# Loading queries, keys and values of a head pair as nine flat chunks, in a fused attention and two-layer feed-forward kernel

## The chip, the cores and the metric

One core of one Trainium2 chip. The metric is the device time of one execution in microseconds; the median of several runs is given.

Names used below: PE is the matrix engine (TensorE), PEld its loading of weights, DVE the vector engine, ACT the scalar engine, POOL the GpSimd engine, SP the engine whose queue issues all transfers (DMA) of this kernel. SBUF is the on-chip memory, PSUM the accumulators that PE writes.

## The reference

Block-causal attention over 4 batches, 8 heads, 576 tokens and head size 64 (blocks of 64 tokens), then two feed-forward layers over the 2304 tokens (512 to 2048 to 512 features):

```python
scores = scale * np.matmul(q, k.transpose(0, 1, 3, 2))
scores = np.where(block_i >= block_j, scores, -1000000000.0)
attn = np.exp(scores - max); attn = attn / (sum + 1e-09)
x = (attn @ v), heads side by side                      # 2304 x 512
h = x @ w_in;  g = max(h, 0) + alpha * min(h, 0);  x = g @ w_out
h = x @ w2_in; g = h * sigmoid(1.702 * h);         out = g @ w2_out
```

q, k and v are 32-bit floats. The four weight matrices arrive as 64-bit floats.

## The kernel before, in words

**Precision.** Each 32-bit operand of a matrix product is split into a high part (`hi_part`, line 114, on ACT) and the remainder (`lo_part`, line 117, on DVE or POOL). A layer product is then three products: high x high, low x high, high x low. Weights are narrowed from 64 to 32 bits by one ACT and three DVE instructions (`narrow`, line 137) and then split.

**Attention.** Work goes by `passes` (line 307): a pass is a pair of heads of one batch. Batch 0 is taken in eight passes: first the query group 0 (rows 0 to 319) of its four pairs, then group 1 (rows 320 to 575), so that the first token block of the layers comes early. The twelve pairs of batches 1 to 3 are one pass each, with both groups. Per pass:

- `load` (line 328) fetches rows of q, k and v through `load_rows` (line 319) into the tiles `nat`, where one partition row holds 64 values of the first head and 64 of the second. A full pair takes, for each of q, k and v, one transfer per head (128 KB, line 324) and one for the last 64 rows of both heads (line 326).
- `prep_t` (line 338) transposes 128 rows of both heads at once on PE, into `tp` in PSUM. The first head comes out on partitions 0 to 63, the second on 64 to 127.
- `prep_out` (line 347) splits that: high parts on ACT, low parts on DVE, one instruction per head. For keys, the low part goes to the other half of the partitions. For queries, both parts stay on the head's own half, and once all query parts of the pass are there, two transfers within SBUF (line 383) copy each head's half to the other half, since a score product needs the same query part against the high half and the low half of the keys.
- `prep_v` (line 385) splits v into three 16-bit parts on ACT and POOL.
- `score` (line 426) makes the products `sc`; `soft` (438) the minimum (DVE) and the exponential (ACT); `norm`, `high` (471, POOL) and `rest` (483, DVE) the normalised probabilities as two 16-bit parts `hl`. Line 493 transposes those by a DMA transpose into `pt`, one per pass, group and head: 64 in all.
- `pv` (line 496) multiplies with v by the list `PV` (line 28), one list per group; `pv_out` (518) adds the halves into `x` and stores it.

**Layers.** The first half of layer 1 (8 of 16 feature tiles) runs beside the attention, by token blocks: two of 320 and 256 tokens for batch 0, then six of 288 (`blocks`, line 595). `gemm1` (line 194) and `g2_half` (232) are its products. The rest of layer 1, and layer 2, follow when the attention's buffers have been given up, by blocks of 384 tokens (`gemm1` and `g2`, line 632). Products of `gemm1` and `g2_half` take their PSUM banks in turn from a pool of two, `ps_m`. `warm` (line 575) issues matmuls without a result on one of these two banks, in groups at steps -5 to 27 of the plan, each group ordered behind the PE instruction ahead of it in the plan.

**The order of the work.** Each piece of work is noted with `at(kind, n, fn)` (line 110): a step `n`, and a place, `n + 0.1 * ORDER[kind] + SHIFT[kind]` (line 111). After the program has been built in the order of the steps, `arrange` (line 778) simulates it with a cost per instruction: on each engine the ready instruction with the smallest place goes next. The order found is then fixed for every engine, SP's queue included. `cost` (754) prices compute instructions, lines 817 to 823 price transfers, lines 889 to 895 say how SP and the transfers follow each other. Each engine carries out its order strictly. `SHIFT` (line 44) holds one number per kind of work.

Of the kernel before, what the change touches and what calls it, by code (L numbers as in the profile page):

```python
# [27 lines left out]
PV = [  # L28
# [3 lines left out]
]  # L32
# [23 lines left out]
def kernel(  # L56
# [27 lines left out]
    NG = 6  # L84
    TB = 384
# [101 lines left out]
    gs_ = blk.tile([128, 2 * NA * GRP[0][2]], F32R, name="gs")  # L187
# [29 lines left out]
    def gate_split(key, f, lo):  # L217
        g, n = pend.pop((key, f))

        w, z = (GRP[0][2], f % NA) if key[0] == 0 else (TB, f % NG)  # L220
# [40 lines left out]
    def plan_x(i, n_split):  # L261
        def f(c):
            if c == 0:
                t0, n = blocks[i]
                xl = blk.tile([128, KD, GRP[0][2]], F32R, tag="xlb", name="xlb")[:, :, 0:n]
                xb[0, i] = (st["x", t0 // S][:, :, t0 % S:t0 % S + n], None, xl, n)
            split_x((0, i), blk, 0, pool, slice(c, c + 1))
# [12 lines left out]
    nat = {n: one.tile([128, 5, 2, D], F32, name=f"nat_{n}") for n in "qkv"}  # L280
    vp = [one.tile([128, 5, 7, D], BF16, name=f"vp{i}") for i in range(2)]
# [3 lines left out]
    def hl_part(j, x, m, n, h):  # L285
        o = 128 * (QT[j][4] + x * QT[j][3])
        z = hl[0 if j < 3 else 1]
        return z[h % len(z)][0:m, o:o + n]


    def setup():
# [4 lines left out]
        for t in nat.values():  # L296
            pool.memset(t[64:128, 4], 0.0)
        for t in vp:
            pool.memset(t[:, :, 3, :], 0.0)
# [10 lines left out]

    PART0 = ((0, 320, ((0, 128), (1, 128), (4, 64))), (320, 256, ((2, 128), (3, 128))))
    PART = ((0, 384, ((0, 128), (1, 128), (2, 128))), (384, 192, ((3, 128), (4, 64))))

    def part_of(i, part):
        return (PART0 if i < N0 else PART)[part]

    def load_rows(nm, i, t0, n, c0, tail):
        b, p, _ = passes[i]  # L320
        src = {"q": q, "k": k, "v": v}[nm][b, 2 * p:2 * p + 2]
        c = n // 128
        for h in range(2):
            sp.dma_start(out=nat[nm][:, c0:c0 + c, h], in_=src[h, t0:t0 + 128 * c, :].rearrange("(c p) d -> p c d", p=128))
        if n % 128:
            sp.dma_start(out=nat[nm][0:64, tail], in_=src[:, t0 + 128 * c:t0 + n, :].rearrange("h p d -> p h d"))

    def load(i, nm):
        gs = passes[i][2]
        if len(gs) == 2 or nm == "v" and gs[0] == 1:  # L330
            load_rows(nm, i, 0, S, 0, 4)
        elif nm == "v":
            load_rows(nm, i, 0, 384, 0, 4)
        else:
            t0, n, chunks = PART0[gs[0]]
            load_rows(nm, i, t0, n, chunks[0][0], 4)

    def prep_t(i, nm, part):
        ps = ps_a.tile([128, 512], F32, tag="tv", bufs=2, name="tp")
        st["tp", i, nm, part] = ps  # L340
        o = 0
        for c, m in part_of(i, part)[2]:

            pe.transpose(ps[:, o:o + 128], nat[nm][:, c].rearrange("p h d -> p (h d)"), ident)
            o += m

    def prep_out(i, nm, part):


        t0, n, _ = part_of(i, part)  # L350
        ps = st.pop(("tp", i, nm, part))[:, 0:n]
        if nm == "q":
            if (i, nm) not in st:
                st[i, nm] = two.tile([128, 2, 2, S], F32R, tag="q", name="qs")
            z = st[i, nm]
        elif i < N0:

            p = passes[i][1]
            if part == 0 and p == 0:
                st["k0"] = blk.tile([128, KD, S], F32R, tag="xl0", name="k0")  # L360
            if part == 0:
                st["k0", p] = st["k0"][:, 2 * p:2 * p + 2] if p < KD // 2 else two.tile([128, 2, S], F32R, tag="k", name="k0")
            z = st["k0", p]
        else:
            if (i, nm) not in st:
                st[i, nm] = two.tile([128, 2, S], F32R, tag="k", name="ks")
            z = st[i, nm]
        half = [slice(0, 64), slice(64, 128)]
        t = slice(t0, t0 + n)
        for h in range(2):  # L370
            hi = z[half[h], h, 0, t] if nm == "q" else z[half[h], h, t]
            hi_part(hi, ps[half[h]], -scale if nm == "q" else 1.0)
        for h in range(2):
            if nm == "q":
                dve.scalar_tensor_tensor(out=z[half[h], h, 1, t], in0=ps[half[h]], scalar=-scale,
                                         in1=z[half[h], h, 0, t].bitcast(F32), op0=ALU.mult, op1=ALU.subtract)
            else:
                lo_part(dve, z[half[1 - h], h, t], ps[half[h]], z[half[h], h, t])
        if nm == "q" and part == passes[i][2][-1]:
            z = z.bitcast(F32)  # L380
            t = slice(0, S) if i >= N0 else t
            for h in range(2):
                sp.dma_start(out=z[half[1 - h], h, :, t], in_=z[half[h], h, :, t])

    def prep_v(i, piece):
        n = 5 if passes[i][2][-1] == 1 else 3
        t, src = vp[i % 2], nat["v"]

        part = t[:, 0:n, piece:7 - piece:6 - 2 * piece, :]
        act.activation(out=part, in_=src[:, 0:n], func=ACTF.Copy)  # L390
        pool.tensor_tensor(out=src[:, 0:n] if piece == 0 else t[:, 0:n, 2:5:2, :], in0=src[:, 0:n], in1=part, op=ALU.subtract)
# [34 lines left out]
    def score(n):  # L426
# [4 lines left out]
        for j, off, heads, parts, _ in st[n, "sc"]:  # L431
            q0, m, nk, ch, c0 = QT[j]
            for part in parts:
                for h, (o, k0, n_) in zip(heads, part):
                    for x in range(2):
                        pe.matmul(o, qs[:, h, x, q0:q0 + m], ks[:, h, k0:k0 + n_], start=x == 0, stop=x == 1)
# [46 lines left out]
    def rest(n, h):  # L483
# [9 lines left out]
        sp.dma_start_transpose(out=pt, in_=hl[g][h % len(hl[g])])  # L493
        st[i, g, h] = pt

    def pv(i, g, h):
# [4 lines left out]
        for o, n, c, skip, tiles in PV[g]:  # L501
            first = [QT[j][4] for j in tiles]
            for a, x in (((0, 0), (0, 1), (2, 0)), ((5, 0), (5, 1), (3, 0)))[h]:
# [5 lines left out]
                ops.append((ps[:, o:o + n], t[:, c, a:a + 2].rearrange("p a d -> p (a d)"), mv))  # L509
# [34 lines left out]

    for i in range(len(passes)):
        full = passes[i][2][-1] == 1
# [7 lines left out]
        todo = [(nm, g) for g in passes[i][2] for nm in "kq"]  # L554
        for z, (nm, part) in enumerate(todo):
# [393 lines left out]
```

## Time and profile before

| what | value |
|---|---|
| median of 3 runs | 1120.61 us (1120.26 to 1124.37) |
| the profiled execution, its own time | 1119.54 us |
| its span in the profile | 1117.7 us |
| packets moved by transfers | 238,919, of which 191,984 under 512 bytes |
| bytes moved | 123.59 MB |

How to read the lines of the profile: the page gives busy time per engine, with the share of the span and the number of instructions behind an x. In groups of instructions, a line names the source line, the engine, the operation, output <- input, shapes and a count; then busy time and mean duration in ns; then the idle time just before them and what ended it. In the view of one tile, a line gives the shortest, median and longest duration in ns and the first and last start. In the view in order of time, a line starts with the start and the duration in us. A wait reads "who <- whom: us in total, times, longest us". SPq is SP's queue: the time in which it issues a transfer, which is not the transfer's own time. Tiles: `nat_q`, `nat_k`, `nat_v` are the loaded rows, `tp` the transposes, `qs` and `ks` (or `k`) the split queries and keys, `sc` the scores, `hl` and `pt` the probabilities before and after the transpose, `pv` their product with v, `h` and `x` the layer products.

The profile's strip of 40 equal slices shows the stages (28 us a slice; digits are tenths):

```profile
PE   6556888868989989899999999999999999999998
DVE  6889877768688887678987125851111111111110
PEclk7888989978999999999999999999999999999999
DMA  7878778797878776544555214511001010000000
```

The attention fills the first 16 slices. There PE, DVE and the transfers are all at 5 to 9 tenths, and the clock granted to PE is below full in the first eight. After that PE is at 9 tenths throughout, DVE falls off, and the transfers stop mattering.

### The profile page before, as it was taken

To read this page: it belongs to the slowest core of one execution; us is meant where nothing else is said; L and a number is where in the kernel's file an instruction comes from. 1 tells how busy PE (TensorE), PEld (TensorE's weight loads), DVE (VectorE), ACT (ScalarE), POOL (GpSimd) and SP (SyncE) were. 2 spreads that over 40 slices of the span, in tenths; PEclk is the share of its full clock that TensorE was granted. 3 is DMA by queue.
4 is the path that set the end of the run, shared out by engine and by line. 5 is a ranking of instruction groups with operands and counts; after the bars stand their busy time and mean duration, and the time that the engine had idled before them with its cause. 6 is when DMAs were issued, how large, how long until landed. Compare 5 with 4: busy or idle time off the path is not lost. (4 is left out here: it accounts for less than half of the span.)

```text
span 1117.7 us, 17627 instructions
## 1 busy us (share of the span) xinstructions
PE 1020.0 (91%) x6478; PEld 926.6 (83%) x6478; DVE 608.1 (54%) x1057; ACT 508.3 (45%) x1192; POOL 463.1 (41%) x496
## 2 busy tenths in 40 slices
PE   6556888868989989899999999999999999999998
PEld 3445777757878879799999999999999999999997
DVE  6889877768688887678987125851111111111110
ACT  5555655546565765555554225533223232232222
POOL 3467654635564745553443224442222222222221
PEclk7888989978999999999999999999999999999999
DMA  7878778797878776544555214511001010000000
GB/s 187 179 177 192 172 159 172 150 171 149 162 145 175 146 159 138 139 145 153 188 180 170 85 57 142 184 57 33 25 1 57 1 57 1 29 29 1 29 1 29
DMA packets 238919, 123.59 MB, mean 111 GB/s; under 512 B 191984, under 2 KB 230896, under 8 KB 238832
## 3 DMA queue, kind: packets, MB, share of 16 engines
q1 hardware_dynamic: 238832, 122.46, 45.3%
q8 instruction: 51, 0.84, 0.3%
q14 instruction: 36, 0.29, 0.1%
HBM read 62.66 MB, written 18.87 MB: 73 GB/s over the span
## 5 line engine op out<-in xcount | busy, mean ns | idle before, releaser
L118 POOL TENSOR_TENSOR gs<-g,gs 128x384 fp32r<-128x384 f32 (+3 forms) x208 | 216.6, 1044 | 456.3 <-ACT gs L115 444.8
L202 PE MATMUL h<-xh,wh 128*128 128x384 f32 (+3 forms) x832 | 272.1, 327 | 9.8 <-DVE g L211 6.8
L202 PE MATMUL h<-xh,wl 128*128 128x384 f32 (+3 forms) x832 | 270.8, 325 | 0.0
L214 DVE TENSOR_TENSOR g<-g,h 128x384 f32<-128x384 f32 x96 | 53.2, 554 | 294.8 <-ACT g L213 294.8
L649 PE MATMUL acc<-wh,gs 128*128 128x512 f32 x576 | 194.9, 392 | 0.6 <-DVE o L659 0.6
L202 PE MATMUL h<-xl,wh 128*128 128x384 f32 x576 | 193.1, 335 | 0.0
L202 PEld LDWEIGHTS h<-xh,wh 128*128 128x128 f32 x832 | 156.6, 188 | 17.8 <-DVE g L211 9.4
L202 PEld LDWEIGHTS h<-xh,wl 128*128 128x128 f32 x832 | 157.0, 189 | 0.1
L115 ACT ACTIVATE gs<-g 128x384 fp32r<-128x384 f32 (+3 forms) x208 | 103.4, 498 | 105.5 <-DVE g L214 60.1
L213 ACT ACTIVATE g<-h 128x384 f32<-128x384 f32 x96 | 47.1, 491 | 195.4 <-PE h L202 195.1
L515 PE MATMUL pv<-pt,vp 128*128 128x256 f16 (+2 forms) x1056 | 92.8, 238 | 45.1 <-DMA pt<-hl 43.5
L481 POOL TENSOR_SCALAR hl<-e,stat 64x64 f16<-64x64 f32 (+4 forms) x160 | 106.3, 681 | 63.0 <-DVE stat L469 45.3
L489 DVE SCALAR_TENSOR_TENSOR hl<-e,stat,hl 64x64 f16<-64x64 f32 (+4 forms) x160 | 120.9, 782 | 11.5 <-POOL hl L481 9.9
L649 PEld LDWEIGHTS acc<-wh,gs 128*128 128x128 f32 x576 | 108.1, 188 | 21.1 <-DVE o L659 1.0
L515 PEld LDWEIGHTS <-vp 128*128 128x128 bf16 x1056 | 65.8, 103 | 64.3 <-DMA pt<-hl 36.1
L649 PE MATMUL acc<-wl,gs 128*128 128x512 f32 x288 | 113.7, 395 | 0.0
L202 PEld LDWEIGHTS h<-xl,wh 128*128 128x128 f32 x576 | 108.1, 188 | 4.1
L649 PE MATMUL acc<-gs,wh 128*128 128x384 f32 x384 | 97.5, 334 | 2.0 <-DVE o L659 2.0
L459 ACT ACTIVATE e<-sc,stat 64x64 f32<-64x64 f32 (+4 forms) x160 | 82.7, 519 | 20.7 <-DVE stat L451 15.2
L211 DVE SCALAR_TENSOR_TENSOR g<-g,nalph,h 128x288 f32<-128x288 f32 (+3 forms) x112 | 61.4, 551 | 49.8 <-ACT g L210 48.8
L118 POOL TENSOR_TENSOR wl<-sq,wh 128x512 fp32r<-128x512 f32 x40 | 56.6, 1416 | 68.4 <-ACT wh L115 58.7
L240 PE MATMUL x<-gs,wh 128*128 128x288 f32 (+2 forms) x256 | 76.4, 302 | 4.8 <-DVE g L211 4.7
(67 smaller groups left out, 1694.8 us busy)
## 6 DMA issues: line engine op xcount, KB each, us to landing
rw<-in_moe_w_in_dram SPq DMA_DIRECT2D x32, 512.0 KB, 4.0
rw<-in_moe_w_out_dram SPq DMA_DIRECT2D x32, 512.0 KB, 3.6
qs<-qs SPq DMA_DIRECT2D x24, 288.0 KB, 4.2
o<-xa SPq DMA_DIRECT2D x24, 192.0 KB, 2.9
xl<-xs SPq DMA_DIRECT2D x6, 768.0 KB, 4.7
x2s<-o SPq DMA_DIRECT2D x24, 192.0 KB, 1.9
xl<-x2s SPq DMA_DIRECT2D x6, 768.0 KB, 4.4
out_dram<-o SPq DMA_DIRECT2D x18, 256.0 KB, 2.0
```

The costliest lines, as they stand in the source:

```text
L115: act.activation(out=dst, in_=src, func=ACTF.Copy, scale=scale_)
L118: eng.tensor_tensor(out=dst, in0=src, in1=hi.bitcast(F32), op=ALU.subtract)
L202: pe.matmul(ps, st_[:, sl], mv[:, c], start=z == 0, stop=z == 3 * KD - 1)
L211: dve.scalar_tensor_tensor(out=g, in0=g, scalar=nalph[:, f:f + 1], in1=ps, op0=ALU.mult, op1=ALU.add)
L213: act.activation(out=g, in_=ps, func=ACTF.Sigmoid, scale=1.702)
L214: dve.tensor_tensor(out=g, in0=g, in1=ps, op=ALU.mult)
L240: pe.matmul(ps, oh[:, sl], gh, start=f == 0, stop=False)
L459: act.activation(out=eo, in_=v[:, h] if len(heads) > 1 else v, func=ACTF.Exp, scale=-1.0, bias=stat[0:m, 0, a:a + 1], accum_out=stat[0:m, ...
L481: pool.tensor_scalar(out=o, in0=e, scalar1=r, scalar2=1.0, op0=ALU.mult, op1=ALU.mult)
L489: dve.scalar_tensor_tensor(out=hl_part(j, 1, m, nk, h), in0=es[h][0:m, off:off + nk], scalar=stat[0:m, 2, 2 * a + h:2 * a + h + 1], in1=hl ...
L515: pe.matmul(o, l, r, start=z == 0, stop=z == len(ops) - 1)
L649: pe.matmul(ps, a, b_, start=f == f0 and z == 0, stop=f == NF - 1 and z == 2)
```

## The change

The two heads of a pair lie one behind the other in memory, so their 2 x 576 rows are nine chunks of 128 rows, and the fifth chunk holds the end of the first head and the start of the second.

1. Loads. q, k and v are loaded as such chunks: k and v once, q twice, into the two halves of each partition row of `nat_q`. A transpose of a chunk of q then gives the same 128 queries on partitions 0 to 63 and on 64 to 127. Keys are transposed two chunks at a time. In batch 0 the passes of group 0 load and prepare all keys, and seven of nine chunks of q and v; the passes of group 1 load seven chunks of q and all of v, and no keys.
2. `prep_out`. Queries are split with all 128 partitions in one instruction per part. The two transfers of line 383 are gone. Keys are still split by halves, a half now being the even or the odd chunks.
3. The second head's rows start 64 rows into the fifth chunk. Its probabilities are therefore written 64 columns further on in `hl`, and `PV` has a second list for it.
4. Token blocks are 288 tokens throughout (`TA`); the buffer `gs` is smaller.
5. `arrange` prices transfers anew: time on SP, time of the packets and a landing time, by run length and by kind, with a DMA transpose holding SP for a time that grows with its size.
6. `SHIFT` has new numbers for every kind of work, and the steps of the loads follow the transposes that free their tiles.

```diff
-PV = [
+PV = [[
     [(0, 64, 0, 0, (0,)), (64, 256, 0, 0, (1, 2)), (128, 64, 1, 64, (1,)), (192, 128, 1, 0, (2,)), (256, 64, 2, 64, (2,))],
     [(0, 256, 0, 0, (3, 4)), (0, 256, 1, 0, (3, 4)), (0, 256, 2, 0, (3, 4)), (64, 64, 3, 64, (3,)), (128, 128, 3, 0, (4,)),
      (192, 64, 4, 64, (4,))],
-]
+], [
+    [(0, 64, 0, 0, (0,)), (64, 256, 0, 0, (1, 2)), (64, 256, 1, 0, (1, 2)), (192, 128, 2, 0, (2,))],
+    [(0, 256, 0, 0, (3, 4)), (0, 256, 1, 0, (3, 4)), (0, 256, 2, 0, (3, 4)), (0, 256, 3, 0, (3, 4)), (128, 128, 4, 0, (4,))],
+]]
...
 SHIFT = {
-    "gate": -13.8, "gate 2": 48.4, "gemm1": 60, "gemm1 2": 60, "gemm2": 60, "half": 60, "half out": -58.4,
-    "high": -53.6, "load alpha": 58.5, "load k": 20.6, "load q": 56.4, "load v": 60, "load w": -11,
-    "load w 2": -60, "load x": 46.3, "narrow": 54.9, "narrow 2": 7.4, "norm": -50, "out": -20.2,
-    "prep out": 24.8, "prep t": -17.9, "prep v": 17.6, "pv": -8.2, "pv out": 35.6, "rest": 50.5, "score": -46.6,
-    "setup": 28.7, "soft": -24.9, "split g": 20.9, "split g 2": 3.7, "split w": -48.5, "split w 2": 60,
-    "split x": 29.2, "split x 2": -44.7, "warm": 9.6,
+    "gate": -44.2, "gate 2": -23, "gemm1": 56.7, "gemm1 2": 12.5, "gemm2": 12.8, "half": 58.9, "half out": -42,
+    "high": -6.3, "load alpha": 27.7, "load k": 56.1, "load q": -37.1, "load v": -27.1, "load w": -32.6,
+    "load w 2": -53.5, "load x": -33, "narrow": 56.5, "narrow 2": -25.1, "norm": -46.2, "out": -53.7,
+    "prep out": 42.4, "prep t": 41.2, "prep v": 41.6, "pv": -10, "pv out": -41.9, "rest": 40.6, "score": 51.7,
+    "setup": -24.2, "soft": 19, "split g": -43.8, "split g 2": 4.8, "split w": 7.8, "split w 2": -28.1,
+    "split x": 26.4, "split x 2": 57.1, "warm": 56.9,
 }
...
     def load(i, nm):
+        b, p, gs = passes[i]
+        src = {"q": q, "k": k, "v": v}[nm][b, 2 * p:2 * p + 2].rearrange("h t d -> (h t) d").rearrange("(c p) d -> p c d", p=128)
+        if nm == "q":
+            c = slice(0, 9) if len(gs) == 2 else (slice(0, 7), slice(2, 9))[gs[0]]
+            for y in range(2):
+                sp.dma_start(out=nat["q"][:, c, y], in_=src[:, c])
+        elif nm == "v" or gs[0] == 0:
+            c = slice(0, 9 if nm == "k" or gs[-1] == 1 else 7)
+            sp.dma_start(out=nat[nm][:, c], in_=src[:, c])
...
+    CH = ((0, 1, 2, 3), (4, 5, 6, 7)), ((0, 1, 2), (4, 5, 6)), ((2, 3, 4), (7, 8))
...
+        if what == "k":
+
+            ts = [nat["k"][:, c:c + 2] for c in range(0, 8, 2)]
+        elif what == "tail":
+            ts = [nat["k"][:, 8:10]] + [nat["q"][:, 8]] * (len(passes[i][2]) == 2)
         else:
...
+            ts = [nat["q"][:, c] for c in chunks(i, what)]
+        for z, t in enumerate(ts):
+            pe.transpose(ps[:, 128 * z:128 * z + 128], t.rearrange("p c d -> p (c d)"), ident)
...
-        if nm == "q" and part == passes[i][2][-1]:
-            z = z.bitcast(F32)
-            t = slice(0, S) if i >= N0 else t
-            for h in range(2):
-                sp.dma_start(out=z[half[1 - h], h, :, t], in_=z[half[h], h, :, t])
...
+        hi_part(z[:, 0, t], y, -scale)
+        dve.scalar_tensor_tensor(out=z[:, 1, t], in0=y, scalar=-scale, in1=z[:, 0, t].bitcast(F32), op0=ALU.mult, op1=ALU.subtract)
...
-        todo = [(nm, g) for g in passes[i][2] for nm in "kq"]
+        todo = ["k", "q0", "q1", "tail"] if passes[i][2][0] == 0 else ["q0", "q1"]
...
-    blocks = [(0, 320), (320, 256)] + [(288 * i, 288) for i in range(2, 2 * B)]
+    blocks = [(TA * i, TA) for i in range(2 * B)]
...
-                c = (450 if list(a.ap)[0][1] > 64 else 625, size / 360 * (1 if min(dma_run(z) for z in ins + outs) >= 512 else 2))
+                run = min(dma_run(z) for z in ins + outs)
+                t = size / run * (8.3 + 0.0368 * run) / 16
+                inside = all(z.tensor.space != DRAM and not z.tensor.name.startswith("in_") for z in ins + outs)
+                c = (580 if inside else 400 if run > 512 else 500, 2 * t if inside else t, 1000 if outs[0].tensor.space == DRAM or inside else 1600)
             else:
-                c = (625, size / 32768 * 112)
+                c = (0.0046 * size - 100, size / 32768 * 130, 2400 - 0.0046 * size)
...
                 if e == "SP":
-                    t = max(now, dge)
-                    dge = t + c[0] + 60
-                    free[e] = max(now + 50, t)
-                    end = ring_end = max(t + c[0] + 650, ring_end) + c[1]
-                    if kind == "InstDmaTransposeAnt":
-                        dge = end - 877
+                    t = now
+                    free[e] = t + c[0] + 70
+                    end = ring_end = max(t + c[0] + c[2], ring_end) + c[1]
```

More of the change, by code (lines that the diff above doesn't have):

```diff
@@ L279 @@
     mk_l = one.tile([128, 128], BF16, name="mk_l")
-    nat = {n: one.tile([128, 5, 2, D], F32, name=f"nat_{n}") for n in "qkv"}
-    vp = [one.tile([128, 5, 7, D], BF16, name=f"vp{i}") for i in range(2)]
+    nat = {"q": one.tile([128, 9, 2, D], F32, name="nat_q"), "k": one.tile([128, 10, D], F32, name="nat_k"),
+           "v": one.tile([128, 9, D], F32, name="nat_v")}
+    vp = [one.tile([128, 9, 4, D], BF16, name=f"vp{i}") for i in range(2)]
     hl = [[one.tile([128, 128 * g[3]], F16, name=f"hl{j}{x}") for x in range(NHL[j])] for j, g in enumerate(GRP)]
@@ L295, in setup @@
         pool.memset(mk_l, 0.0)
-        for t in nat.values():
-            pool.memset(t[64:128, 4], 0.0)
+        pool.memset(nat["k"][:, 9], 0.0)
         for t in vp:
-            pool.memset(t[:, :, 3, :], 0.0)
+            pool.memset(t[:, :, 3], 0.0)
         for t in hl[0] + hl[1]:
@@ L328, in load @@
-    def load(i, nm):
-        gs = passes[i][2]
[L330 to L333, printed above, removed]
-        else:
[L335 to L345, printed above, removed]
@@ new lines, in prep_out @@
+    def prep_out(i, what):
+        ps = st.pop(("tp", i, what))
+        gs = passes[i][2]
+        if what in ("k", "tail"):
+            if i < N0:
+                p = passes[i][1]
+                if what == "k" and p == 0:
+                    st["k0"] = blk.tile([128, KD, S], F32R, tag="xl0", name="k0")
+                if what == "k":
+                    st["k0", p] = st["k0"][:, 2 * p:2 * p + 2] if p < KD // 2 else two.tile([128, 2, S], F32R, tag="k", name="k0")
+                z = st["k0", p]
+            else:
+                if what == "k":
+                    st[i, "k"] = two.tile([128, 2, S], F32R, tag="k", name="ks")
+                z = st[i, "k"]
+            z = z.rearrange("p h t -> p (h t)").rearrange("p (c t) -> p c t", t=128)
+            half = [slice(0, 64), slice(64, 128)]
+            y = ps.rearrange("p (c t) -> p c t", t=128)
+            if what == "k":
+                kinds = [(x, y[half[x]], slice(x, 8, 2)) for x in range(2)]
+            else:
+                kinds = [(0, y[half[0], 0:1], slice(8, 9))]
+            for x, s_, c in kinds:
+                hi_part(z[half[x], c], s_)
+            for x, s_, c in kinds:
+                lo_part(dve, z[half[1 - x], c], s_, z[half[x], c])
+        if what == "k" or what == "tail" and len(gs) == 1:
+            return
+        if (i, "q") not in st:
+            st[i, "q"] = two.tile([128, 2, 2 * S], F32R, tag="q", name="qs")
+        if what == "tail":
+            c0, y = 8, ps[:, 128:256]
+        else:
+            cs = chunks(i, what)
+            c0, y = cs[0], ps[:, 0:128 * len(cs)]
+        t = slice(128 * c0, 128 * c0 + y.shape[-1])
+        z = st[i, "q"]
+        hi_part(z[:, 0, t], y, -scale)
+        dve.scalar_tensor_tensor(out=z[:, 1, t], in0=y, scalar=-scale, in1=z[:, 0, t].bitcast(F32), op0=ALU.mult, op1=ALU.subtract)
@@ L543 @@
                 at("pv out", n + lag + 1 + h, lambda i=i, g=g, h=h: pv_out(i, g, h))
+    used = {}
     for i in range(len(passes)):
-        full = passes[i][2][-1] == 1
         f0 = first[i]
```

92 lines of the change are left out of this document (28 added, 64 removed).

## The prediction

> **What bounds the kernel now.** I read the page first, then a table by stage, then who waits for whom, then the queues.
>
> ```profile
> PE 1020.0 (91%) x6478; PEld 926.6 (83%) x6478; DVE 608.1 (54%) x1057; ACT 508.3 (45%) x1192; POOL 463.1 (41%) x496
> ```
>
> PE is the busiest engine by far, but 91% is an average. The table by stage, with cuts that I chose where the work changes (its columns after the time are PE, PEld, DVE, ACT and POOL busy us, granted TensorE clock, DMA share, GB/s), says where the missing 97.7 us lie:
>
> ```profile
> 0.00:118.00 118.00, 78.19 (x507) 53.39 (x508) 96.15 (x178) 66.72 (x168) 63.50 (x81) 0.83 0.79 181
> 118.00:288.00 170.00, 137.99 (x1103) 122.25 (x1101) 130.85 (x263) 98.42 (x281) 96.94 (x115) 0.92 0.79 160
> 288.00:458.00 170.00, 154.55 (x1353) 141.28 (x1354) 130.68 (x259) 101.60 (x289) 91.84 (x115) 1.00 0.77 155
> 458.00:508.00 50.00, 47.22 (x353) 46.30 (x351) 36.49 (x51) 30.06 (x65) 28.42 (x25) 1.00 0.48 149
> 508.00:1118.00 610.00, 602.07 (x3168) 563.40 (x3167) 213.95 (x308) 211.54 (x392) 182.39 (x162) 1.00 0.21 67
> ```
>
> From 458 us on (the attention is over) PE is busy 649.3 of 660 us, and 508 to 1118 is matrix products alone. The first of those stretches, 50 us, is the two blocks of the last batch, which cannot start before its attention ends. So the time is the end of the attention plus a fixed 660 us, and a microsecond saved or lost before 458 counts in full. Before 458, PE idles 39.8 us in the first stretch, 32.0 in the second and 15.4 in the third.
>
> In the first stretch it is worse than that, since half of the busy time is warm-up:
>
> ```profile
> L580 PE MATMUL warm<-mk_l 128*128 128x384 bf16 x174 | 39.5, 379 | 1.1 <-POOL mk_l L295 1.1
> ```
>
> and in order of time (start us, us):
>
> ```profile
> 116.86 0.98 PE L580 MATMUL warm<-mk_l 128*128 128x384 bf16 x5
> 119.01 0.31 PE L202 MATMUL h<-xh,wh 128*128 128x320 f32 x1
> ...
> 120.77 0.31 PE L202 MATMUL h<-xh,wh 128*128 128x320 f32 x1
> ```
>
> The steady first-layer products begin right behind the last warm-up matmul. The code says why: warm-up holds one of the two banks of `ps_m` until its last group, and that group is ordered behind the products of the sixth pass's probabilities. 118 us is therefore the time of six passes of attention with nothing beside them, 19.7 us each.
>
> What PE waits for (us in total, times, longest us), first before 118 us:
>
> ```profile
> PE pv L515 <- DMA pt<-hl: 20.7, 9, 6.5
> PE sc L436 <- ACT e L459: 4.8, 2, 3.8
> PE tp L344 <- DMA nat_k<-in_k_dram: 4.0, 1, 4.0
> PE sc L436 <- DMA qs<-qs: 3.6, 5, 1.3
> ```
>
> and from 118 to 458 us:
>
> ```profile
> PE pv L515 <- DMA pt<-hl: 22.8, 23, 2.8
> PE sc L436 <- DMA qs<-qs: 7.6, 18, 1.1
> ```
>
> Transfers inside the core (the DMA transposes of the probabilities, and the swaps of the query halves) end most waits. All of them go out through SP's one queue, whose issues last (min, median, max ns):
>
> ```profile
> L383 SPq DMA_DIRECT2D qs<-qs x40: 510/597/1642, 14.5 to 423.7; - x40
> L324 SPq DMA_DIRECT2D nat_q<-in_q_dram x40: 367/472/1325, 3.2 to 398.2; - x40
> L326 SPq DMA_DIRECT2D nat_q<-in_q_dram x16: 607/625/1372, 3.7 to 394.0; - x16
> L324 SPq DMA_DIRECT2D nat_k<-in_k_dram x40: 367/436/908, 1.3 to 392.4; - x40
> L326 SPq DMA_DIRECT2D nat_k<-in_k_dram x16: 607/684/1799, 1.8 to 389.2; - x16
> L324 SPq DMA_DIRECT2D nat_v<-in_v_dram x40: 381/538/1841, 4.4 to 406.1; - x40
> ...
> L326 SPq DMA_DIRECT2D nat_v<-in_v_dram x16: 595/675/1413, 10.6 to 401.2; - x16
> L493 SPq DMA_TRANSPOSE pt<-hl x64: 1282/2630/4094, 34.5 to 452.2; - x64
> ```
>
> Counts by medians: 40 swaps and 168 loads take 23.9 + 18.9 + 10.0 + 17.4 + 10.9 + 21.5 + 10.8 = 113 us of SP, the 64 transposes 168 us: 281 of 458 us before weights and stores. No engine is full (DVE 96.15 of 118 and 77% after, PE 81% and 91%, DMA 0.79), but all are high and every queue is in order.
>
> **The change part by part.**
>
> *Fewer transfers on SP.* A full pair now has 9 loads and 2 swaps, afterwards q twice, k once, v once. In the code that is 12 x 11 + 4 x 10 + 4 x 9 = 208 before and 12 x 4 + 4 x 4 + 4 x 3 = 76 after. At about 0.5 us (between the 0.436 and 0.538 of the three large kinds) 76 cost 38 us, so 75 us leave SP. If an issue grows with its packets (a 288 KB load has 2.25 times those of a 128 KB one), 1.1 us each makes 84, and 30 us leave. I take the first, since 128 KB pieces are issued faster than the 32 KB ones of L326. In the first six passes it is 58 issues against 22, some 20 us less in 118.
>
> *The swap's latency.* One pass of the first stretch:
>
> ```profile
> 49.29 0.53 PE L344 MATMUL tp<-ident,nat_q 128*128 128x128 f32 x3
> ...
> 51.84 1.33 SPq L383 DMA_DIRECT2D qs<-qs  x2
> 51.89 0.49 DVE L375 SCALAR_TENSOR_TENSOR qs<-tp,qs 64x320 fp32r<-64x320 f32 x1
> ...
> 55.78 0.28 PE L436 MATMUL sc<-k,qs 128*64 128x64 f32 x2 [0.75 <-DMA qs<-qs]
> ```
>
> The second low part ends at 52.4, the scores start at 55.8. Without the swap they can follow the low part: up to 3.4 us per pass, 20 us for six. It is not all gain: DVE is busy 96.15 us of the 118, so 100 us is about the floor of this stretch, and the keys of the second group are now prepared in the first four passes, ahead of the warm-up's end. At the start the new shifts put both loads of q, that of v and two of weights ahead of the first keys, for which PE waits 4.0 us now; one weight load and parts of k and q stood there before, so some two issues more, 1 us, against the first swap saved. I take 118 to 106, **-12 us**; bounds 0 (DVE sets the pace) and -18.
>
> *118 to 458 us.* The waits for swaps (7.6) go; what is late next is DVE's low part, which wrote the swap's source anyway, so nothing is left of them. Of the 22.8 us for the transposes I take about half, 12: SP is freer by roughly a quarter and the plan now prices an issue that blocks SP, but the transpose's own landing remains. Bounds 0 and 22.8. The clock of 0.92 inflates 138 us of PE work by 11; with denser PE work I take 4, bounds 0 and 11.
>
> *More PE work.* Transposes go from 160 to 12 x 14 + 4 x 11 + 4 x 5 = 232, and each second head's product list trades two 64-column products for one of 256 columns, three times per group. In 288 to 458 us:
>
> ```profile
> L515 PE MATMUL pv<-pt,vp 128*128 128x256 f16 x176 | 29.5, 274 | 5.8 <-DMA pt<-hl 5.7
> ...
> L515 PE MATMUL pv<-pt,vp 128*128 128x64 f16 x216 | 15.8, 193 | 0.0
> ...
> L344 PE MATMUL tp<-ident,nat_k 128*128 128x128 f32 x27 | 4.9, 280 | 0.0
> L344 PE MATMUL tp<-ident,nat_q 128*128 128x128 f32 x27 | 4.9, 273 | 0.0
> ```
>
> A transpose takes 9.8 / 54 = 0.181 us of PE. 24 of the 72 added ones lie in batch 0, under the dead time of the first stretch; the other 48 cost **+8.7**. A wide product takes 0.168 and a narrow one 0.073: 16 pairs x 2 x 3 x 0.022 = **+2.1**.
>
> *What costs nothing.* DVE and ACT treat the same columns of q and k per full pair, 128 rows deep and in three instructions rather than four; V is 576 columns rather than 640, which shortens POOL's and ACT's work, neither of which is full. Blocks of 320 + 256 become 288 + 288: the same columns. The new shifts reorder the late stage too; its PE idles 8 of 610 us, so there is nothing to gain there; DVE at 214 of 610 covers it, and if the new order breaks that cover I allow the same 8 us again as a loss, in the range only.
>
> Sum: -12 - 7.6 - 12 - 4 + 8.7 + 2.1 = -24.8, a span of 1092.9. The profiled execution took 1119.54 beside its span of 1117.7 (1.8 around it), 1.1 under the median of 1120.61. So 1092.9 + 2.9 = about **1095 us**.
>
> *The packets.* Per pair a swap moves runs of up to 4.6 KB, while a row of q is 256 bytes. By the code, loads grow from 58,368 such rows to 82,432, and 9,216 KB of swaps go.
>
> ```profile
> q1 hardware_dynamic: 238832, 122.46, 45.3%
> ```
>
> and, for the landing of a DMA transpose (median us from issue),
>
> ```profile
> pt<-hl SPq DMA_TRANSPOSE x64, 4.6
> ```
>
> The first row gives 16 x 1117.7 x 0.453 = 8101 us of single engines: 33.9 ns per packet, 67.7 ns per KB. The added 24,064 packets are at most 51 us over 16 engines, the swaps 39 us by bytes, or nearly nothing if long runs are cheap. The DMA share before 458 us moves from 0.78 to between 0.81 and 0.89. The sum above has 0 for it, since no transfer engine is full at either.
> The Trainium skill speaks against this part ("DMA: Bandwidth & Descriptors", "Why small descriptors are slow (HBM only)"): small pieces pay a fixed overhead when they come from HBM, and transfers within SBUF do not. By that rule the worse end, 0.89, holds; no row of this trace separates the two kinds.
>
> **The rivals.**
> - *Slower: the attention loses its head start on PE.* In the plan before, a score stands 46.6 steps early and a first-layer product 60 late; afterwards they are at 51.7 and 56.7, and the transposes move from -17.9 to 41.2. If one group of 12 products (119.01 to 120.77 is 1.76 us at 320 columns, so 1.58 at 288) stands ahead of the transposes and of the scores of each pair and the chain has no slack, 12 x 2 x 1.58 = 38 us return: 1133. It decides once the chain of a pair, about 28 us in 340 / 12, has less than 3 us of slack. For it: 458 is followed by a fixed 660. Against: PE at 81% and 91% waits for the chain's transfers now, not the chain for PE.
> - *No change: DVE keeps the pace*, or the large issues are slow: the first stretch gives 4, the transposes' waits stay, swaps' waits and added PE work remain: -4 - 7.6 + 10.8 = -0.8, so 1120. For it: DVE at 81% of the first stretch.
> - *Transfers become the limit:* at a share of 0.89 each of the 48 transposes of the full pairs lands later by (0.89 - 0.78) / 0.78 of the 2.0 us between the end of its issue and its landing (4.6 - 2.63), or 0.28 us: 13 us, so 1108. For it: the share is 0.77 to 0.79 in all three stretches. Against: bytes fall on balance, by 9.2 MB of swaps against 6.2 MB of rows.
> - *All of it:* -18 - 7.6 - 22.8 - 11 + 10.8 = -48.6, so 1072.
>
> **How the numbers follow.** Forecast 0.46, on its own 1080 (the waits for `pt` all gone, -11, and more of the clock, -4) to 1108 (half the first stretch's gain and half of the 12 us, +12); all of it 0.18; transfers 0.08; no change 0.12; slower 0.16. A difference under 0.5% (5.6 us) can't be told from none here. The first three lie under 1115: faster 0.72, same 0.12, slower 0.16. The range leaves out the slower case and a little below 1072: 1066 to 1127.
>
> **What would show it.** Right: steady first-layer products start near 106 us; no wait for `qs`; `nat` issues near 0.5 us; waits for `pt` from 118 to the attention's end about 11 us; the attention ends near 433 and 660 us follow; `tp` 15 us more of PE. Wrong: first-layer products still at 118 with DVE full; waits of DVE and ACT for `tp` and `sc` that grow; PE gaps in the late stage; or a DMA share near 0.9 with landings of `pt` well over 4.6 us.

## The result and the profile after

| | before | after |
|---|---|---|
| median | 1121.69 us (4 runs, 1120.26 to 1124.37) | 1086.31 us (4 runs, 1084.72 to 1087.43) |
| profiled execution, its span | 1119.54, 1117.7 | 1087.33, 1085.5 |

The ratio is 0.968, with a 95% interval of 0.9655 to 0.9706: 35 us faster. The forecast was 1095, with a range of 1066 to 1127. Of the variants below, `e_swaps_late` has a time but no usable profile: the one execution that was profiled took 2011 us, the nine others 1118 to 1123.

The table by stage for the changed kernel, cut where the last warm-up group starts and where the last product with v starts (same columns as in the prediction):

```profile
0.00:112.60 112.60, 81.49 (x519) 56.38 (x520) 92.29 (x172) 62.52 (x160) 63.54 (x81) 0.86 0.85 190
112.60:421.50 308.90, 285.13 (x2397) 264.55 (x2395) 256.87 (x500) 191.40 (x549) 189.22 (x226) 0.99 0.84 163
421.50:1086.00 664.50, 654.79 (x3543) 613.32 (x3540) 255.09 (x358) 240.75 (x457) 209.68 (x188) 1.00 0.23 73
```

and the kernel before, with the same two cuts:

```profile
0.00:117.50 117.50, 77.69 (x504) 52.92 (x505) 95.65 (x178) 66.25 (x167) 63.00 (x81) 0.83 0.79 182
117.50:458.10 340.60, 293.14 (x2459) 264.09 (x2457) 262.02 (x522) 200.50 (x570) 189.28 (x229) 0.96 0.78 158
458.10:1118.00 659.90, 649.18 (x3519) 609.61 (x3516) 250.44 (x358) 241.60 (x456) 210.81 (x187) 1.00 0.23 74
```

The first stretch is 4.9 us shorter, the second 31.7. The rest runs to the span's end: 1117.7 - 458.1 = 659.6 before and 1085.5 - 421.5 = 664.0 after, 4.4 longer. That makes up the 32.2 us between the two spans. Nearly all of the gain is in the second stretch: there PE's idle time fell from 47.5 to 23.8 us and its busy time from 293.1 to 285.1, while the granted clock rose from 0.96 to 0.99. The busy time did not vanish: it rose by 3.8 us in the first stretch and by 5.6 in the last, where 24 more of PE's instructions now stand, so over the whole kernel it is 1.4 us longer.

What PE waits for in the changed kernel, in the second stretch:

```profile
PE pv L519 <- DMA pt<-hl: 6.4, 7, 2.2
PE sc L441 <- ACT e L464: 5.2, 9, 1.3
PE h L207 <- ACT xo L251: 3.2, 4, 1.1
PE x L245 <- ACT wh L120: 2.4, 1, 2.4
```

The wait for swaps is gone, and the wait for transposed probabilities (`pt`) went from 22.8 to 6.4 us. These are 7.6 + 16.4 = 24.0 us of waits, and PE's idle time in this stretch fell by 23.7. What is late next is small and spread over several engines. In the first 112 us it is the loads, DVE and small things:

```profile
PE tp L345 <- DMA nat_k<-in_k_dram: 5.1, 3, 2.6
PE pv L519 <- DMA pt<-hl: 4.2, 2, 4.0
PE tp L345 <- DVE stat L473: 3.7, 1, 3.7
PE tp L345 <- DMA nat_q<-in_q_dram: 3.5, 2, 2.5
```

The wait for `pt` fell here as well, from 20.7 to 4.2 us, and the swaps' 3.6 us are gone, yet the stretch is only 4.9 us shorter. Other waits took their place, those for DVE above all: all of them together went from 0.6 to 9.8 us. The waits for `nat_k` and `nat_q` were there before (4.0 us, and the line below) and grew only from 6.7 to 8.6.

```profile
PE tp L344 <- DMA nat_q<-in_q_dram: 2.7, 1, 2.7
```

SP's issues in the changed kernel (min, median, max ns):

```profile
L322 SPq DMA_DIRECT2D nat_q<-in_q_dram x40: 368/454/3537, 0.7 to 365.1; - x40
...
L325 SPq DMA_DIRECT2D nat_k<-in_k_dram x16: 367/399/713, 2.4 to 359.3; - x16
...
L325 SPq DMA_DIRECT2D nat_v<-in_v_dram x20: 367/493/1712, 1.2 to 363.8; - x20
...
L498 SPq DMA_TRANSPOSE pt<-hl x64: 1274/2670/4946, 28.3 to 413.9; - x64
DMA to landing us min/median/max: 3.6/4.6/8.3
```

There are 76 loads with medians of 0.40 to 0.49 us (45.2 us in all). By the medians, a load of 288 KB takes SP no longer than one of 128 KB did, as assumed. A transpose still lands after 4.6 us, although the share of the transfer engines in the second stretch rose from 0.78 to 0.84.

PE's own work, the three groups that the change touches, before and after:

```profile
L515 PE MATMUL pv<-pt,vp 128*128 128x256 f16 (+2 forms) x1056 | 92.8, 238 | 45.1 <-DMA pt<-hl 43.5 <-DVE g L211 0.7 <-DVE x L528 0.6
...
L344 PE MATMUL tp<-ident,nat_q 128*128 128x128 f32 x80 | 17.0, 315 | 2.1 <-DVE ks L118 1.9 <-PE sc L436 0.2
L344 PE MATMUL tp<-ident,nat_k 128*128 128x128 f32 x80 | 16.1, 303 | 7.4 <-DMA nat_k<-in_k_dram 4.0 <-DMA nat_q<-in_q_dram 2.7 <-PE sc L436 0.5
```

```profile
L519 PE MATMUL pv<-pt,vp 128*128 128x256 f16 (+2 forms) x960 | 88.1, 248 | 14.6 <-DMA pt<-hl 10.5 <-DVE x L532 1.6 <-DVE k L123 0.8
...
L345 PE MATMUL tp<-ident,nat_q 128*128 128x128 f32 x152 | 27.6, 290 | 12.8 <-DVE stat L473 3.7 <-DMA nat_q<-in_q_dram 3.5 <-issue 2.5
...
L345 PE MATMUL tp<-ident,nat_k 128*128 128x128 f32 x80 | 15.3, 292 | 6.3 <-DMA nat_k<-in_k_dram 5.1 <-DVE x L532 0.8 <-DVE qs L388 0.2
```

The 72 more transposes cost 42.9 - 33.1 = 9.8 us, and the products with v, 96 fewer and wider, take 4.7 us less rather than more. Both sums hold a share of the higher granted clock.

### The profile page after: what moved, and what is told of

Same layout as the page of the kernel before. It is cut to its first block, busy times and chain, and to the rows that moved or that the text cites. A ratio compares the mean times of both kernels' runs of the same rounds, so it can differ in the third digit from the quotient of the medians.

```text
span 1085.5 us, 17180 instructions
## 1 busy us (share of the span) xinstructions
PE 1021.4 (94%) x6454; PEld 934.3 (86%) x6454; DVE 604.3 (56%) x1029; ACT 494.7 (46%) x1164; POOL 462.4 (43%) x494
## 5 line engine op out<-in xcount | busy, mean ns | idle before, releaser
L123 POOL TENSOR_TENSOR gs<-g,gs 128x384 fp32r<-128x384 f32 (+1 forms) x208 | 212.8, 1024 | 452.4 <-ACT gs L120 431.8
L207 PE MATMUL h<-xh,wh 128*128 128x384 f32 (+1 forms) x832 | 272.2, 327 | 6.8 <-ACT xo L251 3.7
L207 PE MATMUL h<-xh,wl 128*128 128x384 f32 (+1 forms) x832 | 270.2, 325 | 0.0
L120 ACT ACTIVATE gs<-g 128x384 fp32r<-128x384 f32 (+1 forms) x208 | 103.3, 498 | 106.7 <-DVE g L219 60.9
L519 PE MATMUL pv<-pt,vp 128*128 128x256 f16 (+2 forms) x960 | 88.1, 248 | 14.6 <-DMA pt<-hl 10.5
L464 ACT ACTIVATE e<-sc,stat 64x64 f32<-64x64 f32 (+4 forms) x160 | 82.8, 520 | 34.0 <-DVE hl L494 19.2
L216 DVE SCALAR_TENSOR_TENSOR g<-g,nalph,h 128x288 f32<-128x288 f32 (+1 forms) x112 | 61.6, 551 | 58.4 <-ACT g L215 57.4
L123 POOL TENSOR_TENSOR wl<-sq,wh 128x512 fp32r<-128x512 f32 x40 | 59.5, 1488 | 61.7 <-ACT wh L120 61.6
L245 PE MATMUL x<-gs,wh 128*128 128x288 f32 x256 | 75.7, 302 | 2.9 <-ACT wh L120 2.4
```

The source lines that it names most:

```text
L120: act.activation(out=dst, in_=src, func=ACTF.Copy, scale=scale_)
L123: eng.tensor_tensor(out=dst, in0=src, in1=hi.bitcast(F32), op=ALU.subtract)
L207: pe.matmul(ps, st_[:, sl], mv[:, c], start=z == 0, stop=z == 3 * KD - 1)
L216: dve.scalar_tensor_tensor(out=g, in0=g, scalar=nalph[:, f:f + 1], in1=ps, op0=ALU.mult, op1=ALU.add)
L245: pe.matmul(ps, oh[:, sl], gh, start=f == 0, stop=False)
L464: act.activation(out=eo, in_=v[:, h] if len(heads) > 1 else v, func=ACTF.Exp, scale=-1.0, bias=stat[0:m, 0, a:a + 1], accum_out=stat[0:m, ...
```

## The experiments

Two theories at the start. **D**, the data path: the gain comes from what is no longer done (swaps in front of the scores, small transfers on SP). **P**, the plan: it comes from the new shifts and transfer prices, which place each instruction where its transfer has landed. A third question was what sets the length of the first stretch. "Old" and "new plan" below mean shifts and prices together. Each ratio is to the kernel before on the same chip at the same time, where it took 1121.7 to 1123.7 us.

| kernel | median us | ratio (95%) | last warm-up starts | last product with v starts |
|---|---|---|---|---|
| before | 1121.7 | 1 | 117.5 | 458.1 |
| after | 1086.3 | 0.968 (0.9655 to 0.9706) | 112.6 | 421.5 |
| e_old_plan | 1098.4 | 0.979 (0.9756 to 0.9819) | 115.7 | 424.4 |
| e_before_new_plan | 1158.7 | 1.033 (1.0289 to 1.0360) | 140.0 | 492.2 |
| e_swaps | 1166.8 | 1.040 (1.0369 to 1.0437) | 145.0 | 498.5 |
| e_swaps_old_plan | 1169.3 | 1.041 (1.0380 to 1.0440) | 140.8 | 509.3 |
| e_swap_by_part | 1162.8 | 1.036 (1.0334 to 1.0385) | 131.5 | 494.6 |
| e_swap_by_part_old_plan | 1141.6 | 1.018 (1.0155 to 1.0196) | 137.5 | 477.6 |
| e_swaps_late | 1120.6 | 0.997 (0.9960 to 0.9987) | no profile | no profile |
| e_split_loads | 1098.9 | 0.979 (0.9765 to 0.9823) | 115.5 | 430.2 |
| e_head_start | 1102.1 | 0.981 (0.9786 to 0.9833) | 117.9 | 428.6 |
| e_jitter | 1107.2 | 0.987 (0.9850 to 0.9888) | 128.3 | 443.0 |
| e_short_warm | 1093.6 | 0.975 (0.9731 to 0.9768) | 68.2 | 421.3 |
| e_no_narrow | 1081.8 | 0.964 (0.9621 to 0.9657) | 116.0 | 412.4 |

### Plan and data path exchanged

`e_old_plan` is the changed kernel with the `SHIFT` table and the transfer prices of the kernel before; `e_before_new_plan` is the kernel before with those of the changed kernel. Core of the first edit:

```diff
-                c = (580 if inside else 400 if run > 512 else 500, 2 * t if inside else t, 1000 if outs[0].tensor.space == DRAM or inside else 1600)
+                c = (450 if list(a.ap)[0][1] > 64 else 625, size / 360 * (1 if min(dma_run(z) for z in ins + outs) >= 512 else 2))
...
-    "gate": -44.2, "gate 2": -23, "gemm1": 56.7,
+    "gate": -13.8, "gate 2": 48.4, "gemm1": 60,
```

> The changed kernel's data path (nine-chunk loads, queries twice, no swaps, blocks of 288) with the shifts and the transfer prices of the kernel before; nothing of the computation differs. Theory D (the data path gives the gain: swaps and 132 transfers gone from SP): most of the 35 us stays, 1086 to 1100. Theory P (the plan gives it: new shifts and prices put each instruction where its transfer has landed): the gain is lost, 1115 to 1135, with waits for pt back near 20 us after the first stretch.

> The kernel before (swaps, nine loads per pair, blocks of 320 and 256) with the shifts and the transfer prices of the changed kernel. Theory D: it stays within 10 us of 1121, since swaps and small loads are still there. Theory P: it comes down to 1090 to 1105, with the waits for pt falling as they did in the changed kernel (27 to 10 us less).

Measured: 1098.4 and 1158.7. The data path under the old plan keeps 24 of the 35 us; the new plan alone, on the old data path, loses 36. Theory P falls as the main cause: its plan is worse than the old one for a kernel that swaps. That it does something for the new data path (12 us) is measured against the control below.

### The swaps put back

In the changed kernel both halves of the partitions hold the same queries, so a swap can be put back that writes what is there already. In `e_swaps` it stands in `prep_out`, behind the last query part and ahead of the scores:

```diff
+        if what == ("tail" if len(gs) == 2 else "q1"):
+            swap(i)
...
+    def swap(i):
+        z = st[i, "q"].bitcast(F32)
+        gs = passes[i][2]
+        t0, n = (0, S) if len(gs) == 2 else GRP[gs[0]][1:3]
+        for h in range(2):
+            c = slice(S * h + t0, S * h + t0 + n)
+            sp.dma_start(out=z[64 - 64 * h:128 - 64 * h, :, c], in_=z[64 * h:64 * h + 64, :, c])
```

> The changed kernel with the two swap transfers of each pass put back ahead of the scores (they write the values that are there already, so the output is the same), planned with the new prices. Theory D: 40 more issues (24 us of SP), 9.4 MB more and the swap's landing in front of every score cost 15 to 25 us: 1100 to 1112. Theory P: the plan works around them, 1086 to 1093.

`e_swaps_old_plan` is the same under the old plan:

> The changed data path with the swaps put back ahead of the scores, and the shifts and prices of the kernel before (it differs from the run with the old plan by the swaps alone; they write values that are there already). If the swap is dear by itself (its issue, its bytes and its landing in front of the scores), it costs 15 to 25 us here too: 1113 to 1123. If it was dear only because the new plan gives the scores no head start, it costs under 8 us here: below 1106.

Measured: 1166.8 and 1169.3, that is 80 and 71 us over the kernels without swaps, far more than either theory expected. Part of it may be this edit: cut by head, in a tile that has the head inside the part, the second transfer overlaps the first in the planner's rectangles, and under the old plan the order of SP's queue showed 5.7 us between the two issues of the first pass (at 15.61 and 21.29 us). So the swap was cut by part instead, both transfers from the lower to the upper half, with the same bytes and the same number of issues:

```diff
+        for x in range(2):
+            w = z[:, x].rearrange("p (h t) -> p h t", t=S)[:, :, t0:t0 + n]
+            sp.dma_start(out=w[64:128], in_=w[0:64])
```

> As the run with the swaps put back, with the new plan, but the two transfers of a pass are cut by part (high, low) rather than by head: both copy partitions 0 to 63 to 64 to 127, so that neither has rows in common with the other, which the earlier cut had and which put the second swap behind the first in the plan. The same bytes and the same number of issues; the output is unchanged. If the 80 us were mostly the swaps' own cost: still over 1140. If half of it or more was the two swaps one after the other: 1100 to 1130.

> The same swaps by part, with the shifts and prices of the kernel before; to be set against 1098 without swaps. Theory D (swap issue, bytes and landing in front of the scores are the main cost of the kernel before): 1113 to 1128, close to the 1122 of the kernel before. If the small loads are what costs: below 1108. If the earlier cut was no matter: 1160 or more.

Measured: 1162.8 and 1141.6, so 76 us over the changed kernel and 43 over `e_old_plan`. The earlier cut cost 28 us under the old plan, but only 4 under the new one, so it was the cause of little there. The expected 15 to 30 us were too few, and the new plan suffers more from a swap than the old. The kernel so made is not the kernel before, though: under the old plan it is 20 us slower than that one, which swaps too. So the 43 us are what a swap costs in this data path; they are not the swaps' share of the 35 us gained. The waits of PE in `e_swap_by_part`:

```profile
PE pv L529 <- DMA pt<-hl: 29.6, 25, 5.0
PE sc L451 <- ACT e L474: 15.6, 9, 3.1
PE sc L451 <- DMA qs<-qs: 12.8, 13, 2.3
```

The swap's own wait is only 12.8 us. The wait for `pt` is back at 29.6, from 10.5 in the changed kernel, though a transpose lands hardly later (a median of 4.8 us against 4.6). A pass whose scores are late has its probabilities late, so a swap could show up under the name of the transposes. The old plan does not bear this out as a rule. In `e_swap_by_part_old_plan` the swap's own wait is the longest, and the wait for `pt` is what it was in `e_old_plan` (the third line):

```profile
PE sc L451 <- DMA qs<-qs: 17.5, 24, 3.0
PE pv L529 <- DMA pt<-hl: 14.2, 10, 4.5
PE pv L519 <- DMA pt<-hl: 13.4, 13, 2.8
```

What both plans have in common stands in the first line of the pages: the same 6454 instructions keep PE busy some 25 us longer with the swaps, at a lower granted clock. First the new plan without and with swaps (clock 0.982 and 0.954), then the old plan (0.984 and 0.954):

```profile
PE 1021.4 (94%) x6454; PEld 934.3 (86%) x6454; DVE 604.3 (56%) x1029; ACT 494.7 (46%) x1164; POOL 462.4 (43%) x494
PE 1046.2 (90%) x6454; PEld 951.5 (82%) x6454; DVE 623.3 (54%) x1029; ACT 496.1 (43%) x1164; POOL 452.4 (39%) x494
PE 1019.2 (93%) x6454; PEld 933.5 (85%) x6454; DVE 594.4 (54%) x1029; ACT 498.9 (46%) x1164; POOL 464.8 (43%) x494
PE 1044.8 (92%) x6454; PEld 950.1 (84%) x6454; DVE 614.5 (54%) x1029; ACT 496.8 (44%) x1164; POOL 462.0 (41%) x494
```

So of the 76.5 and 44.5 us between the spans, some 25 each are busy time of PE at the lower clock, and 52 and 19 are idle time of PE.

`e_swaps_late` has the 40 transfers (cut by head) behind the last scores of their pass, where no score waits for them:

```diff
+        at("prep out", first[i + 1] - 1, lambda i=i: swap(i))
```

> The changed kernel with the 40 swaps issued behind the last scores of their pass, so that SP and the transfer engines carry them but no score waits for them. If the 80 us that the swaps cost ahead of the scores are latency in the chain, little of it is left: 1088 to 1100. If they are SP's time and the transfers' bytes, most of it is: over 1120.

Measured: 1120.6, 34 us over the changed kernel. This is on the edge of the second expectation, though 34 of 80 us is not most of it. Behind the scores the swaps cost 46 us less than ahead of them in the same cut (1166.8). So more than half of their price in this cut hangs on their place ahead of the scores. The other 34 include SP's time, the bytes, a query tile that is given up later, and the change of plan as such, which the control prices; these were not separated.

### A control, and three changes that turn out no larger

`e_jitter` moves every shift by 2, up and down in turn (`"gate": -42.2, "gate 2": -25.0, "gemm1": 58.7, ...`).

> The changed kernel with every shift moved by 2 steps, up and down in turn; no other change. A control: if an arbitrary small change of the plan costs 8 us or more (1094 to 1102), then the 12 to 16 us that the split loads, the head start and the old plan cost each are no more than the loss of a plan fitted to this kernel. If it costs under 5 us, they are effects of their own.

Measured: 1107.2, 21 us over the changed kernel. A change that means nothing costs that much, and most of it shows in the first stretch, which ends at 128.3 rather than 112.6. So the plan is fitted closely to this kernel, and a loss of up to about 20 us in any other variant can't be put down to what was edited. It is one control, and only under the new plan. Without any swap it has twice the changed kernel's wait for `pt`, 22.6 us against 10.5, so a rise of that wait is no mark of a swap either:

```profile
PE pv L519 <- DMA pt<-hl: 22.6, 15, 4.1
```

`e_split_loads` cuts every load into pieces of three chunks, 228 issues rather than 76:

```diff
+            for a in range(c.start, c.stop, 3):
+                e = slice(a, min(a + 3, c.stop))
+                sp.dma_start(out=nat[nm][:, e], in_=src[:, e])
```

> The changed kernel with every load cut into pieces of three chunks (12 transfers per full pair rather than 4, the same bytes and packets), planned with the new prices. Theory D, the part on SP's issues: some 140 more issues of 0.45 us, 60 us of SP, cost 10 to 20 us: 1096 to 1106. If the issues' number matters little: 1086 to 1091.

`e_head_start` gives the scores and the transposes their early places back:

```diff
-"prep t": 41.2
+"prep t": -17.9
...
-"score": 51.7
+"score": -46.6
```

> The changed kernel with two of the shifts as they were: score -46.6 (from 51.7) and prep t -17.9 (from 41.2), so that PE takes attention work as soon as it can. If the lost head start costs time in the changed kernel (the slower rival of the prediction in part): 1070 to 1083. If not, the same within 8 us, or slower, since the other shifts go with the late scores: 1083 to 1100.

Measured: 1098.9 and 1102.1, so 12.6 and 15.8 us over the changed kernel and both under the control. Neither shows an effect of its own. Giving the head start back brings nothing, so the lost head start costs the changed kernel nothing that can be seen. The kernel with split loads falls in the range that theory D named for them (1096 to 1106), but a new plan alone can cost as much. So that part of theory D, the number of issues, is neither shown nor excluded.

### What sets the first stretch, and whether it matters

`e_no_narrow` leaves out three DVE instructions for each of the first sixteen weight tiles:

```diff
+        if u[0] == 0 and u[1] < NA:
+            words[u] = sq
+            return
         a = raw.tile([128, 512], I32, tag="wa", bufs=1, name="wa")
```

> The changed kernel without the three DVE instructions that narrow each of the first sixteen weight tiles (the low bits of those weights are left out and their exponents stay wrong, so the output is not the reference's): some 36 us less DVE work, all of it before about 150 us. If DVE sets the pace of the first stretch (92 of 112 us busy), the steady first-layer products start at 98 to 104 us rather than 112.7, and the total falls by about as much. If the chain of latencies sets it, they start at 109 or later.

Measured: 1081.8, with the last warm-up at 116.0, so the second of the two expectations. Its first stretch and the waits in it:

```profile
0.00:116.00 116.00, 82.18 (x519) 56.03 (x520) 72.42 (x142) 68.71 (x170) 62.85 (x85) 0.87 0.94 214
```

```profile
PE tp L348 <- DMA nat_k<-in_k_dram: 10.2, 4, 3.6
PE tp L348 <- DMA nat_q<-in_q_dram: 9.9, 4, 6.1
```

With DVE at 72 of 116 us the stretch is not shorter, so DVE is not what alone sets its pace. The loads are what PE waits for now, with the transfer engines at 0.94. The attention still ends 9 us earlier than in the changed kernel, at 412.4, and the total falls by 4.5. Whether that comes from the 14 us less of DVE work behind the first stretch or from the new plan is open, since both are below the control.

`e_short_warm` ends the warm-up earlier:

```diff
-    W3 = 28
+    W3 = 14
```

> The changed kernel with the warm-up groups ending at step 13 of the plan rather than 27. If the first-layer products of batch 0 wait for nothing but the warm-up's bank, they start steadily near 60 to 75 us rather than at 112.7, 20 to 26 us of PE work move into the dead time, and the total falls by 8 to 25 us: 1061 to 1078. If weights or the attention's chain hold them, or a lower clock takes it back, it stays within 8 us of 1086.

Measured: 1093.6, 7 us over the changed kernel and so the second of the two expectations. In its order of time the first-layer products start steadily at 68.6 us, as the bank explanation says, 44 us earlier than in the changed kernel. The table over the stretches that follow, and the last product with v:

```profile
60.00:90.00 30.00, 21.06 (x140) 15.91 (x140) 27.45 (x48) 17.37 (x42) 19.69 (x21) 0.79 0.85 192
90.00:112.00 22.00, 21.34 (x171) 20.17 (x170) 19.78 (x34) 14.96 (x38) 19.90 (x20) 1.00 0.77 163
112.00:140.00 28.00, 17.42 (x107) 13.74 (x105) 24.65 (x37) 15.86 (x41) 16.66 (x15) 0.76 0.91 191
140.00:168.00 28.00, 19.82 (x140) 17.59 (x141) 23.15 (x47) 14.05 (x40) 11.63 (x15) 0.82 0.85 186
```

```profile
L519 PE MATMUL pv<-pt,vp x960: 190/272/437, 34.7 to 421.3; 128*128 128x256 f16 x108, 128*128 128x64 f16 x63, 128*128 128x128 f16 x21
```

PE is full from 90 to 112 us and then idles at a lower clock until 168 us; the changed kernel was busy 26.0 and 19.2 us in the last two of these stretches, at a clock of 1.00 and 0.94. I read it as work that was only moved forward. The attention ends at 421.3, against 421.5. So filling PE's dead time early gained nothing here. That the attention's own chain of passes sets its end fits this, but the lower clock and the new plan, the other reasons why a gain could be lost, were not taken out.

## Why the prediction was right, and where it was off

- **Direction and size: right, the parts less so.** 1086 against 1095 (the sum itself gives 1095.8), inside the forecast's own range of 1080 to 1108. By stretch the forecast was -12, -12.8 and 0; the spans show -4.9, -31.7 and +4.4. That the total is nearer than its parts is luck: the errors of the first and the last stretch took back part of that of the second. The rivals "no change" and "slower" did not come about.
- **The waits in the second stretch: right.** 7.6 us for the swaps and 12 for `pt` were to go, 19.6 in all; 7.6 and 16.4 went, and PE's idle time fell by 23.7.
- **PE's work: the term that was off most.** +10.8 us in the second stretch, with -4 for the clock, was to be +6.8; PE's busy time there fell by 8.0. That is 14.8 of the 18.9 us by which this stretch was missed. 9.4 us of PE's work now stand in the other two stretches, which the forecast had no term for. Over the whole kernel PE's busy time rose by 1.4: the transposes cost 9.8 us rather than 13.0, the products with v took 4.7 less rather than 2.1 more, and the clock's rise from 0.96 to 0.99 is worth some 9 us of 293 by my estimate (293 x 0.03 / 0.99).
- **The swaps as the cause: right; their price is not their wait.** Under both plans the changed kernel loses its whole gain when it swaps ahead of the scores, by 43 to 80 us, while PE waits only 12.8 and 17.5 us for the swaps themselves (cut by part). Some 25 us of the rest are PE's own work at a lower clock. Where the remaining idle time is booked differs with the plan. How much of the 35 us is the swaps' alone stays open, since the kernels with swaps put back are not the kernel before.
- **SP's freed time: neither shown nor excluded as a cause.** 75 us were to leave SP. Added up over the single issues in the traces, loads and swaps went from 130.4 to 45.2 us, the transposes from 151.2 to 159.5, and all issues from 367.5 to 292.5: 75 us. The run with the loads split has 116.2 us of loads again and costs no more than the control.
- **The transfers' share: the right number for another reason.** It was to go from 0.78 to between 0.81 and 0.89 because the new rows add 12 to 51 us to 458. It went to 0.84 and 0.85, but the transfers took no longer: queue q1 was busy, as a mean of the 16 transfer engines, for 0.453 x 1117.7 = 506 us before and 0.461 x 1085.5 = 500 after. The same work stands in a shorter time. The rule of the Trainium skill that small pieces from HBM pay an overhead and transfers within SBUF do not (on the page "DMA: Bandwidth & Descriptors", section "Why small descriptors are slow (HBM only)") stood behind the worse end, 0.89. This case does not follow that end. The 40 swaps put back by part bring q1 to 0.475 x 1162.0 = 552 us, 52 more, so a swap is far from "nearly nothing". A `pt` lands after 4.6 us as before, and the transfers did not become the limit.

```profile
q1 hardware_dynamic: 257200, 119.18, 46.1%
q1 hardware_dynamic: 261424, 128.62, 47.5%
```

- **The first stretch: off, and its reason is not borne out.** It was to go from 118 to 106, with DVE as a floor at 100. It went to 112.6, and without 20 us of its DVE work it is no shorter. The waits for `pt` and the swaps fell by 20.1 us, but PE's idle time only by 8.7, as waits for DVE (9.8 us) and others came up. What brought these is open: that all keys are now loaded and prepared in the first four passes, and that the loads are larger, are only argued, since no run undid one of them alone. The swaps, put back, make the stretch 131.5 to 145.0 long, but the control alone makes it 128.3.
- **"A microsecond before 458 counts in full": not quite.** The attention ended 36.6 us earlier and the span 32.2. After the attention 664.0 us follow (660 forecast), 4.4 more: not a lost cover, but 5.6 us of PE's work that now stands there. And `e_short_warm` took PE's dead time before the end of the attention and gained nothing.
- **The plan.** The prediction gave the plan no term of its own. The old plan on the new data path costs 12 us, a jitter of the new one 21, so the plan's worth can't be told from the loss of any plan that is not fitted. Five variants have no swaps and such a plan (`e_no_narrow` with its missing work left aside). They lie between 1093.6 and 1107.2; those with swaps ahead of the scores between 1141.6 and 1169.3. Neither of the two plans closes that gap, so it goes with the swaps. The kernel before, with swaps and a plan fitted to them, lies in it at 1121.7.

## What to carry to other kernels

A wait that bears a step's name is not the price of that step in a serial chain: 12.8 and 17.5 us of waits stood beside 76 and 43 us of time. The latency times the number of passes is a second estimate to set beside it: the prediction read 3.4 us for a swap in one pass, and 20 passes of it are 68 us by estimate. Where a planner's order has been fitted to one kernel, compare variants with a control that changes the order and nothing else, here 21 us, before a loss is put down to an edit. And an idle engine is worth filling only if its work sets the end.

## What the runs showed of the hardware that was not expected

- With the swaps put back, PE's same 6454 instructions took some 25 us longer, at a granted clock of 0.954 rather than 0.982 and 0.984. In the stretches of `e_short_warm` the clock goes with PE's busy share: 1.00 at 97%, 0.79 and 0.82 at 70 and 71%, 0.76 at 62%. So a wait may cost twice, as idle time and as slower work around it.
- A DMA transpose holds SP longer than a load does, 1.27 to 4.95 us with a median of 2.67. The size seems to be one reason: in the changed kernel the first eight, of group 0 (12 tiles of 128 columns), took 1.43 to 2.58 us, the next eight, of group 1 (18 tiles), 2.70 to 3.66. Over all 64 it was 151.2 us in the kernel before, 159.5 in the changed one, and 147.7 with the loads split. These are sums of the single issues, which the view in order of time does not always show:

```profile
180.96 4.95 SPq L498 DMA_TRANSPOSE pt<-hl  x1
186.00 0.53 SPq L534 DMA_DIRECT2D xs<-x  x1
186.64 9.79 SPq L498 DMA_TRANSPOSE pt<-hl  x2
```

The last row is two issues, of 3.95 and 1.27 us, with 4.56 us between them in which SP issued nothing. A row that merges several issues holds the time between them, and a sum of such rows is too large.

- The issue time of a load on SP does not grow with its packets: medians of 0.40 to 0.49 us for 224 to 288 KB, and 0.44 to 0.54 us for 128 KB in the kernel before.
- The 40 swaps within SBUF, 9.4 MB, took some 52 us averaged over the 16 transfer engines (552 less 500 us of q1), more than the 39 us estimated for their bytes.
